# A scan on VectorE for the running sums of log f, key rows copied by DMA, and a new order of the first words, in a fused attention and GELU kernel

## The chip, the cores and the metric

The kernel runs on one core of one Trainium2 chip. The metric is device time in microseconds (us) of one execution. The core has TensorE (PE in the profile, with PEld for its weight loads), VectorE (DVE), ScalarE (ACT), GpSimd (POOL) and SyncE (SP); DMA transfers are issued from the queues of SP, ACT and POOL.

## What is computed

Attention with a decay for 8 batches of 8 heads, 576 positions and 64 dimensions, and behind it a two-layer MLP with the tanh form of GELU over 4608 tokens (512 to 2048 to 512):

```python
log_f = np.log(np.clip(f, 0.0001, 1.0))
cum = np.cumsum(log_f, axis=-1)
scores = scale * q @ k.T + cum[..., :, None] - cum[..., None, :]   # causal
attn = softmax(scores) @ v
x = attn as (tokens, heads * dims)
out = gelu_tanh(x @ w_in) @ w_out
```

Since the softmax divides out what depends on the query alone, the kernel needs of `cum` only exp(-cum) of the keys. It multiplies the values by that weight (`vw`) and uses the weights themselves as the columns of the denominators (`w_bf`).

## The kernel before, in words

Sixteen quads (4 heads of one batch each) run through attention, two quads a batch. For a quad the loads of queries and keys (`LQ.i`, `LK.i`, line 208, on POOL's queue, cast to bf16) are followed by a 32x32 block transpose on DVE (`TQ.i`, `TK.i`, line 214). `S.i.r` or, for two heads, `H.i.r.g` are the score products of a round of columns (line 277, contraction over 32 rows) and their exponentials on ACT (line 285), through two PSUM tiles of the pool psS. `M` masks on POOL (line 291), `m` by a product on DVE (line 321). `VW` and `vw` weight the values (line 231) on POOL or DVE. `D.i` are the denominators (products at lines 333 and 347, then a transpose, a reciprocal and a transpose back on DVE, lines 366 to 370), `V.i.x` and `v.i.x` the products with the values and their division into `xT` (line 379). The first two quads are split into query parts; the third number of their words says which.

From the third quad on, 64 key rows stand in an extra block named LOW: `CL.i` (`copy_low`, line 236) copies rows 0 to 63 of block 0 of `vw` to rows 64 to 127 of block LOW. V reads that block as its second.

The MLP goes by nine chunks of 512 tokens. `I`, `i`, `J` and `j` are whole products with `w_in` (lines 395 and 419), 16 matmuls to a J; `GJ` the GELU that a j left over. `Q`, `E` and `e` are products of sums (Strassen's scheme) with sums from `T`, `UW`, `PW` and `U`. `F.c.n` and `f.c.n` pull n steps of the products with `w_out`: for chunk 0 a step is one block of 128 rows by 512 columns (line 667), for later chunks of 256 columns (line 600). F issues a step as one matmul over the full 128 columns of the array, f as four matmuls over 32 columns each. Results go to DRAM by SP's queue.

`WI.c` and `WO.c` load the pieces of `w_in` and `w_out` (lines 197 and 201) on POOL's queue; J.x.g needs WI.2g and WI.2g+1, and an F of chunk 0 passes through WO.0 to WO.3 in turn. `LP` and `LC` load value tiles on POOL's queue (line 185), `LV` and `LB` on SP's. `B.n.c` is filler: n matmuls of c columns over zeros into an unused tile (line 256). `X` and `Y` load ACT's tables for exp and GELU. `Z` and `TR` or `tr` set zeros and the two causal triangles.

The order of the work on every engine is written out by hand: `run` goes through tables of such words, `SETUP` and `FRONT` once (quads 0 to 6 and chunks 0 and 1 in part), then `SECOND`, `STEADY`, `FLUSH` and `LAST` for the chunks from 2 on, with the quad number moved on by two a chunk. Each engine and each DMA queue takes its instructions in this order; a word with `@` waits for another word's load.

Running sums before: `setup` (from line 677) loads f as 64 rows of 576, clips it on DVE (line 694), takes Ln on ACT (line 695), transposes the five blocks on PE (line 700) and copies them from PSUM to `logfT` on ACT (lines 702 and 703). The word `CW` (`make_w`) then multiplies by a triangle of ones (line 719, within a block) and adds whole blocks by products with ones (line 721), all in fp32, and ACT takes exp(-cum - 64) into `wT` (line 724). `W` casts `wT` to `w_bf` on DVE (lines 748 and 749).

Of the kernel before, what the change touches and what calls it, by code (L numbers as in the profile page):

```python
# [16 lines left out]
def kernel(  # L17
# [49 lines left out]
    LOW, HIGH = NT, NT - 1  # L67
# [4 lines left out]
        TK.0 LP.0 LP.1  # L72
# [74 lines left out]
    f_sb = f_all[0:BH, :]  # L147
# [87 lines left out]
    def copy_low(i):  # L235
        return nc.vector.tensor_copy(vw[i % 2][64:128, LOW], vw[i % 2][0:64, 0])
# [440 lines left out]
    def setup():  # L677
# [10 lines left out]
        nc.vector.memset(logfT, 0.0)  # L688
# [28 lines left out]
    def make_w():  # L717
        cum_ps = psM.tile([128, NT * BH], FP32, name="cum_ps", tag="m")
        nc.tensor.matmul(cum_ps, utri_f32, logfT, start=True, stop=True)
        for n in range(NT - 1, 0, -1):  # L720
            nc.tensor.matmul(cum_ps[:, n * BH:], ones_f32, logfT[:, :(NT - n) * BH], start=False, stop=True,  # L721
                             skip_group_check=True)
        for (rows, t0, t1) in ((128, 0, HIGH), (64, HIGH, NT)):
            nc.scalar.activation(
                wT[:rows, :, t0:t1, :].rearrange("p i t h -> p t i h"),
                cum_ps[:rows, t0 * BH:t1 * BH].rearrange("p (t i h) -> p t i h", i=NQ, h=4),
                AF.Exp, scale=-1.0, bias=shift[:rows, :])
# [131 lines left out]
```

## Time and profile before

| | |
|---|---|
| median of 3 runs | 323.59 us (323.31 to 323.96) |
| profiled execution | 323.22 us |
| its span, first to last instruction | 321.4 us |
| PE, ACT, DVE, POOL busy | 309.6, 212.7, 242.0, 107.8 us |
| granted TensorE clock | 1.00 |

Busy time is the time in which an engine had an instruction in it. Matmuls are pipelined, so the distance from one start to the next says what a matmul costs PE, not its own length. In a row of the timeline stand the start, the length, the engine, the line, the operation, output and input tiles, how many instructions are in the row and, in brackets, how long the engine stood idle before it and what ended that. In the windows each engine's busy time is followed by its instructions, then come the granted clock, the DMA share and GB/s. In the rows of groups, busy time and the mean in ns are followed by the idle time before them. In the rows of DMA issues the last number is the median time from issue to landing in us.

### The profile page before, as it was taken

How to read it: one execution, taken by the hardware profiler on the slowest of the kernel's cores; microseconds unless marked ns; L12 is line 12 of the kernel's file. 1: busy time of each engine (PE TensorE's matmuls, PEld its weight loads, DVE VectorE, ACT ScalarE, POOL GpSimd, SP SyncE). 2: the span in 40 equal slices, each digit the busy share in tenths (PEclk: the TensorE clock that was granted, in tenths of full speed). 3: DMA queues.
4: the chain of work that ended last, by engine and by line, in shares of the span. 5: the costliest groups of instructions: out<-in, count | busy, mean ns of one | idle time of the engine just before them, and what ended most of it. 6: DMA issues, size and time to landing. Idle time of an engine off the chain costs nothing.

```text
span 321.4 us, 11820 instructions
## 1 busy us (share of the span) xinstructions
PE 309.6 (96%) x5339; PEld 220.7 (69%) x5339; DVE 242.0 (75%) x374; ACT 212.7 (66%) x242; POOL 107.8 (34%) x145
## 2 busy tenths in 40 slices
PE   0899999999999999999999999999999999999996
PEld 0557844544776567776788878767776786688785
DVE  4765337898979879779877987699876866597674
ACT  4676576775766776878767866787586744836610
POOL 8989343522301416400851075205610140000000
PEclk9999999999999999999999999999999999999999
DMA  7999999585126931593139411971011111010203
GB/s 126 218 210 208 247 213 199 104 155 109 35 43 129 227 78 37 116 209 72 39 82 228 87 39 35 190 172 36 7 47 53 37 34 37 30 37 0 100 33 99
DMA packets 47490, 33.41 MB, mean 104 GB/s; under 512 B 29776, under 2 KB 42192, under 8 KB 47440
## 3 DMA queue, kind: packets, MB, share of 16 engines
q0 software_dynamic: 9632, 15.99, 28.3%
q1 hardware_dynamic: 37664, 16.60, 19.1%
q8 instruction: 41, 0.67, 0.9%
q14 instruction: 9, 0.07, 0.1%
q10 hardware_dynamic: 144, 0.07, 0.1%
HBM read 36.85 MB, written 9.44 MB: 144 GB/s over the span
## 4 chain that ended last, share of the span: by engine, by line
PE 91%; ACT 3%; DVE 3%; DMA 2%; issue 1%; POOL 0%; DVEq 0%; POOLq 0%
PE ps_w L600 30%; PE ps_h L395 19%; PE ps_s L277 9%; PE po L347 9%; PE ps_q L520 8%; PE pso L667 4%; PE ps_h L419 4%; PE ps_u L468 4%; DMA q_c<-in_q_dram 2%; PE po_m L333 1%; ACT pt L285 1%; ACT gT L403 1%; DVE xT L379 1%; PE idle_ps L256 1%; PE cum_ps L721 1%
## 5 line engine op out<-in xcount | busy, mean ns | idle before, releaser
L285 ACT ACTIVATE pt<-ps_s 128x1024 bf16<-128x1024 f32 (+2 forms) x100 | 94.0, 990 | 38.6 <-PE ps_s L277 35.9
L291 POOL TENSOR_SCALAR_AFFINE_SELECT pt<-pt 128x512 bf16<-128x512 bf16 (+3 forms) x65 | 41.4, 647 | 95.2 <-ACT pt L285 72.3
L395 PE MATMUL ps_h<-xT,w_in_sb 128*128 128x512 bf16 (+1 forms) x320 | 66.8, 358 | 0.3 <-ACT gT L403 0.2
L395 PEld LDWEIGHTS <-w_in_sb 128*128 128x128 bf16 x320 | 31.2, 98 | 26.6 <-issue 0.6
L600 PEld LDWEIGHTS <-gT 128*32 128x32 bf16 (+1 forms) x1216 | 44.1, 97 | 5.5 <-issue 2.2
L403 ACT ACTIVATE gT<-ps_h 128x1024 bf16<-128x1024 f32 x34 | 34.6, 1017 | 18.7 <-PE ps_h L395 18.4
L600 PE MATMUL ps_w<-w_out_sb,gT 128*32 128x256 bf16 (+1 forms) x1008 | 42.6, 273 | 0.0
L277 PE MATMUL ps_s<-qT,kT 32*128 32x64 bf16 (+5 forms) x896 | 36.3, 263 | 3.2 <-DVE qT L214 3.0
L600 PEld LDWEIGHTS <-gsum 128*32 128x32 bf16 (+1 forms) x948 | 35.4, 97 | 3.8 <-issue 1.5
L231 POOL TENSOR_TENSOR vw<-v_nat,wT 128x1280 bf16<-128x1280 f32 (+1 forms) x13 | 29.6, 2279 | 11.7 <-DMA v_nat<-in_v_dram 11.4
L536 DVE TENSOR_TENSOR usnap<-ps_q,usnap 128x1024 f32<-128x1024 f32 x15 | 17.9, 1222 | 18.6 <-PE ps_q L520 13.2
L277 PEld LDWEIGHTS <-kT 32*128 32x128 bf16 x896 | 16.5, 93 | 19.6 <-issue 10.1
L600 PE MATMUL ps_w<-usum,gsum 128*32 128x256 bf16 (+1 forms) x791 | 30.0, 273 | 0.0
L617 DVE COPY snap<-ps_w 128x512 f32<-128x512 f32 x32 | 21.8, 681 | 6.2 <-PE ps_w L600 6.0
L531 ACT ACTIVATE gT<-usnap 128x1024 bf16<-128x1024 f32 x15 | 15.8, 1054 | 12.1 <-DVE usnap L536 11.8
L379 DVE TENSOR_TENSOR xT<-po,rb 128x576 bf16<-128x576 f32 x26 | 19.5, 752 | 5.6 <-PE po L347 5.3
L347 PE MATMUL po<-pt,vw 128*32 128x64 bf16 (+4 forms) x624 | 22.4, 278 | 0.0
L214 DVE STREAM_TRANSPOSE qT<-q_c 128x576 f32<-128x576 f32 x16 | 19.8, 1246 | 1.7 <-DMA q_c<-in_q_dram 1.7
L347 PEld LDWEIGHTS <-vw 128*32 128x32 bf16 x672 | 14.6, 97 | 9.4 <-issue 2.8
L214 DVE STREAM_TRANSPOSE kT<-k_c 128x576 f32<-128x576 f32 x16 | 19.5, 1246 | 1.9 <-DMA k_c<-in_k_dram 1.9
L208 POOL DMA_DIRECT2D k_c<-in_k_dram x16 | 9.1, 568 | 33.6 <-DVE kT L214 18.0
L520 PEld LDWEIGHTS <-w_in_sb 128*128 128x128 bf16 x160 | 15.6, 98 | 2.5 <-issue 0.4
(135 smaller groups left out, 478.5 us busy)
## 6 DMA issues: line engine op xcount, KB each, us to landing
out_dram<-o_st SPq DMA_DIRECT2D x35, 256.0 KB, 2.3
k_c<-in_k_dram POOLq DMA_DIRECT2D x16, 288.0 KB, 5.3
q_c<-in_q_dram POOLq DMA_DIRECT2D x16, 288.0 KB, 6.3
v_nat<-in_v_dram SPq DMA_DIRECT2D x16, 256.0 KB, 5.4
v_nat<-in_v_dram SPq DMA_DIRECT2D x20, 128.0 KB, 5.1
v_nat<-in_v_dram POOLq DMA_DIRECT2D x8, 256.0 KB, 8.1
w_in_sb<-in_moe_w_in_dram POOLq DMA_DIRECT2D x8, 256.0 KB, 7.8
w_out_sb<-in_moe_w_out_dram POOLq DMA_DIRECT2D x4, 512.0 KB, 11.3
```

What stands on the lines that cost most here:

```text
L214: return nc.vector.transpose(out=dst.rearrange("p s c -> p (s c)").bitcast(FP32) .rearrange("p (t a) -> p a t", a=S // 32), in_=src.rearra ...
L231: return eng.tensor_mul(vw[i % 2][:, t0:t1], vb[:, t0:t1, h0:h0 + 4, :], wT[:, i, t0:t1, :].unsqueeze(3).to_broadcast([128, t1 - t0, 4, D]))
L277: nc.tensor.matmul(tiles[h // 2][:, h % 2, c0:c0 + nq], key_columns(i, key, h, c), qq[32 * h:32 * h + 32, q0:q0 + nq, c], start=(c == 0 an ...
L285: nc.scalar.activation(p[:, 2 * g:2 * g + 2, off:off + n], t[:, :, 0:n], AF.Exp, scale=scale)
L291: nc.gpsimd.affine_select(out=x, in_=x, compare_op=ALU.is_ge, fill=0.0, base=0, pattern=pattern, channel_multiplier=-1)
L347: nc.tensor.matmul(po[r0:r0 + w.shape[-1], 448 + q0:448 + q0 + nq], w, p[:, h, col:col + nq], start=(key in (0, "low")), stop=(key in ("lo ...
L379: nc.vector.tensor_mul(xT[:, 2 * u + x, r0 + s0:r0 + s1], po, rbs[i, part])
L395: nc.tensor.matmul(ph[:, j, n * cols:(n + 1) * cols], w_in_sb[:, dt, 128 * ft:128 * ft + 128], xT[:, dt, h0:h0 + cols], start=(dt == 0 and ...
L403: nc.scalar.activation(gelus(c, 2 * pr, 2), ph, AF.Gelu_apprx_tanh)
L520: nc.tensor.matmul(ps[:, k, HC * n:HC * n + HC], w[:, d, 128 * n:128 * n + 128], x[:, d, :], start=(first and n == 0 and d == 0), stop=(d ...
L600: nc.tensor.matmul(ps[c0:c0 + width, n, cols[0]:cols[1]], x[:, j, 128 * n + c0:128 * n + c0 + width], w[:, j, cols[0]:cols[1]], start=(fir ...
L617: copy(kept[name], ps)
```

## The change

Three things change.

1. Running sums: behind Ln one `tensor_tensor_scan` on DVE multiplies the state by one and adds the next element, along the 576 positions of the 64 rows. `CW` becomes the five transposes of the summed rows into PSUM and the same two exponentials on ACT. The ACT copies to `logfT`, its memset and the fp32 products go. `CW` moves into `SETUP`, ahead of the first key transpose.
2. `copy_low` becomes a DMA issued by SP, in every table that has `CL`.
3. `FRONT` has another order. Among it: `TR` on DVE becomes `tr` on ACT; several masks change between POOL and DVE, `VW.1.1` goes to DVE and `vw.2` to POOL; three `UW.2` sums on DVE become `PW.2` on POOL; filler goes from 10 matmuls (3,968 columns) to 30 (8,960 columns); the loads stand in another order and the words with `@` become fewer; F and f steps are split otherwise, with 38 steps of chunk 0 as F before and 40 after, of chunk 1 35 and 22, the sums of F and f being the same (64 and 97).

```diff
     SETUP = """
-        TK.0 LP.0 LP.1
+        CW TK.0 LP.0 LP.1
     """
     FRONT = """
-        Z TQ.0 LP.2 TR WI.1 TQ.1 S.0.0 B.1.384 CW WI.0 TK.1 S.0.2 LP.4 LP.3 B.1.512 vw.0.0 B.2.512 H.1.0.1 H.1.1.1 WI.3 M.0.0 W vw.1.0 WI.2 B.2.512
-        WI.5 LQ.2 WI.4 H.1.0.0 D.0.0 M.1.0.1 M.1.0.0 H.0.1.1 V.0.0.0 H.0.1.0 M.0.1 WI.6 V.0.1.0 B.2.256 H.1.1.0 B.1.256 D.1.0 H.0.3.0 B.1.256 V.1.0.0 H.0.3.1
-        WI.7 LK.2 V.1.1.0 m.0.3.2 H.1.3.0 j.0.0 vw.0.1 H.1.3.1 LC.1.4 WO.0 m.0.3.4 WO.1 D.0.1 M.1.3 S.1.2 M.1.1 VW.1.1 V.0.0.1 V.0.1.1 LC.1.2 D.1.1
-        J.0.1 J.0.2 WO.2 LC.1.0@VW.1.1 WO.3@m.0.3.2 V.1.0.1 V.1.1.1 LC.1.1 GJ.0.0 LC.1.3 TK.2 J.1.1 LK.3 J.0.3 J.1.0 LQ.3 TQ.2 LQ.4 VW.3
-        J.1.3 LK.4 J.1.2 F.0.4 X F.0.4 S.2.0 F.0.11 TK.3 S.2.2 F.0.6 LV.2.0 TQ.3 F.0.4 LK.5 S.2.1 F.0.2 F.0.7 TQ.4 m.2.1 S.3.0 vw.2 CL.2 M.2.2 f.0.7
-        M.2.0 D.2 S.3.1 f.0.7 LQ.5 V.2.0 m.3.0 S.3.2 TK.4 LK.6@LQ.4 f.0.1 f.0.3 V.2.1 M.3.2 f.0.2 S.4.1 CL.3 m.3.1 LQ.6 f.0.5 TQ.5 H.4.2.1 D.3 H.4.0.1
-        H.4.0.0 VW.4 V.3.1 v.3.0 f.0.1 H.4.2.0 U.0 m.4.1 LV.2.1@m.3.1 I.1.1 LQ.7@CL.3 I.1.4 TQ.6 I.1.6 m.4.2.3 I.1.0 m.4.2.2 I.1.5 CL.4 U.3 LV.3.0@LQ.7
-        U.1 TK.6 I.1.2 M.4.0 U.2 G.0 TK.5 UW.2.1 I.1.3 I.1.7 G.1.1.2 F.1.16 X UW.2.2 S.5.0 UW.2.3 LQ.8 F.1.19 S.5.1 D.4 VW.5 M.5.0 f.1.13 S.5.2 V.4.0
-        f.1.14 V.4.1 UW.2.4 m.5.2.3 m.5.2.2 CL.5 M.5.1 S.6.0 f.1.13 D.5 S.6.1 f.1.4 LK.7 V.5.1 f.1.3 f.1.10 vw.6 S.6.2 m.6.1 M.6.2.2 m.6.0 V.5.0
-        LV.3.1@LK.6 f.1.5 CL.6 LK.8 m.6.2.3
+        B.1.256 B.1.128 TQ.0 S.0.0 TK.1 B.1.128 B.1.256 B.2.512 B.1.128 LP.4 B.1.512 B.1.256 B.1.512 LP.2 LP.3 B.1.128 B.1.512 WI.4 TQ.1 vw.0.0 S.0.2 B.1.128 B.1.128 B.1.128 H.0.1.1 H.1.1.1 WI.6 B.1.128 B.1.128 B.1.256 M.0.0 B.1.512 WI.0 WI.1 H.1.0.1 tr W LC.1.4 D.0.0 V.0.1.0 WI.2 B.2.512 B.1.512 B.1.256 vw.1.0 H.1.0.0 V.0.0.0 B.1.256 B.1.128 B.1.256 m.1.0.0 H.0.1.0 H.1.1.0 m.1.0.1 B.1.512 B.1.128 D.1.0 WI.3 Z V.1.0.0 WI.5 LK.2 H.0.3.0 B.1.512 WO.2 B.1.128 M.0.1 WO.1 WI.7 V.1.1.0 H.0.3.1 vw.0.1 vw.1.1 m.0.3.2 H.1.3.1 LC.1.2 j.0.0 S.1.2 M.0.3.4 D.0.1 m.1.1 V.0.0.1 H.1.3.0 m.1.3 LQ.2 J.0.1 TK.2 GJ.0.0 V.0.1.1 D.1.1 WO.0 J.0.2 V.1.0.1 WO.3 LC.1.1 LC.1.0 V.1.1.1 J.1.2 LC.1.3 J.1.1 LK.3 LQ.3 J.0.3 J.1.0 TQ.2 LQ.4 LK.4 J.1.3 F.0.3 VW.3 f.0.1 F.0.1 X TK.3 F.0.3 S.2.0 F.0.9 S.2.2 TQ.3 F.0.2 CL.3 M.2.0 F.0.8 VW.2 F.0.3 S.2.1 F.0.1 M.2.2 F.0.3 M.2.1 F.0.2 f.0.2 TQ.4 F.0.2 LQ.6 S.3.0 f.0.2 CL.2 LQ.5 X f.0.4 TK.4 D.2 S.3.1 f.0.3 m.3.0 f.0.1 V.2.0 f.0.2 S.3.2 TQ.5 F.0.3 LV.2.0 m.3.1 M.3.2 f.0.2 V.2.1 S.4.1 f.0.5 H.4.2.1 UW.2.1 LK.5 D.3 VW.4 H.4.0.0 H.4.0.1 V.3.1 v.3.0 f.0.1 TK.5 M.4.1 f.0.1 LQ.7 H.4.2.0 TQ.6 U.0 LK.6 I.1.7 I.1.3 I.1.5 I.1.4 I.1.2 m.4.2.3 I.1.0 CL.4 I.1.1 U.3 LV.2.1 I.1.6 TK.6 F.1.5 U.1 m.4.2.2 LV.3.0@LQ.7 PW.2.2 G.0 f.1.1 F.1.5 S.5.0 f.1.13 m.4.0 G.1.1.2 LK.8 f.1.8 VW.5 f.1.4 S.5.1 M.5.1 f.1.4 D.4 f.1.2 F.1.6 S.5.2 V.4.0 f.1.1 m.5.2.3 f.1.4 m.5.2.2 f.1.2 CL.5 f.1.7 LV.3.1 V.4.1 M.5.0 PW.2.3 f.1.1 U.2 S.6.0 f.1.5 D.5 f.1.6 m.6.0 LQ.8 f.1.1 S.6.1 f.1.2 V.5.1 f.1.8 LK.7 f.1.2 S.6.2 M.6.2.2 m.6.1 f.1.3 vw.6 V.5.0 M.6.2.3 f.1.1 F.1.5 PW.2.4 F.1.1 CL.6
     """
...
     def copy_low(i):
-        return nc.vector.tensor_copy(vw[i % 2][64:128, LOW], vw[i % 2][0:64, 0])
+        return nc.sync.dma_start(out=vw[i % 2][64:128, LOW], in_=vw[i % 2][0:64, 0])
...
         nc.vector.memset(ones_f32, 1.0)
-        nc.vector.memset(logfT, 0.0)
...
         nc.scalar.activation(f_sb, f_sb, AF.Ln)
         idle_ps.append(psO.tile([128, 1024], FP32, name="idle_ps", tag="po"))
-        ps_lt = psM.tile([128, NT * BH], FP32, name="ps_lt", tag="m")
-        for t in range(NT):
-            n = min(128, S - 128 * t)
-            nc.tensor.transpose(ps_lt[:n, t * BH:(t + 1) * BH], f_sb[:, 128 * t:128 * t + n], ident_f32)
+        nc.vector.tensor_tensor_scan(f_sb, ones_f32[0:BH, 0:1].to_broadcast([BH, S]), f_sb, 0.0,
+                                     op0=ALU.mult, op1=ALU.add)
         run(SETUP)
-        nc.scalar.copy(logfT[:, :HIGH * BH], ps_lt[:, :HIGH * BH])
-        nc.scalar.copy(logfT[0:64, HIGH * BH:], ps_lt[0:64, HIGH * BH:])
...
     def make_w():
         cum_ps = psM.tile([128, NT * BH], FP32, name="cum_ps", tag="m")
-        nc.tensor.matmul(cum_ps, utri_f32, logfT, start=True, stop=True)
-        for n in range(NT - 1, 0, -1):
-            nc.tensor.matmul(cum_ps[:, n * BH:], ones_f32, logfT[:, :(NT - n) * BH], start=False, stop=True,
-                             skip_group_check=True)
+        for t in range(NT):
+            n = min(128, S - 128 * t)
+            nc.tensor.transpose(cum_ps[:n, t * BH:(t + 1) * BH], f_sb[:, 128 * t:128 * t + n], ident_f32)
```

## The prediction

> **What bounds the kernel now.** I read the page's chain first (section 4), then busy time by stage, then the timelines of PE, ACT, DVE and POOL over the first 41 us, where the change acts. All durations are of the profiled execution (323.22 us, span 321.4); the median of the runs shown is 323.59, 0.37 above it, so what I add to the one I add to the other.
>
> ```profile
> PE 91%; ACT 3%; DVE 3%; DMA 2%; issue 1%; POOL 0%; DVEq 0%; POOLq 0%
> ```
> ```profile
> 12.00:21.00 9.00, 8.73 (x132) 4.01 (x131) 6.75 (x15) 8.15 (x12) 8.40 (x13) 1.00 1.14 207
> ...
> 27.00:41.00 14.00, 14.00 (x166) 12.00 (x159) 4.47 (x7) 7.93 (x9) 7.58 (x10) 1.00 1.20 240
> ```
>
> The chain that ended last is PE for 91%. In the windows (columns: PE, PEld, DVE, ACT, POOL busy, granted clock, DMA share, GB/s) 12 to 21 us is different: ACT works 8.15 of 9 us. That is the start, where sixteen exponentials of the first two quads are waited for; from 27 us on PE is full and DMA is at 240 GB/s. So a microsecond saved ahead of the first MLP products (word j.0.0) counts, one saved on DVE, ACT or POOL later does not, and one added to PE later counts in full.
>
> ```profile
> L285 ACT ACTIVATE pt<-ps_s 128x768 bf16<-128x768 f32 x8 | 6.3, 810 | 3.5 <-PE ps_s L277 3.4
> L285 ACT ACTIVATE pt<-ps_s 128x1024 bf16<-128x1024 f32 x4 | 4.0, 1021 | 0.1
> L285 ACT ACTIVATE pt<-ps_s 128x640 bf16<-128x640 f32 x4 | 2.6, 695 | 0.4 <-PE ps_s L277 0.4
> ```
> ```profile
> 9.47 1.51 ACT L285 ACTIVATE pt<-ps_s 128x768 bf16<-128x768 f32 x2 [2.00 <-PE ps_s L277]
> 12.62 0.67 ACT L724 ACTIVATE wT<-cum_ps,shift 128x256 f32<-128x256 f32 x2 [1.64 <-PE cum_ps L721]
> ```
> ```profile
> 8.62 0.83 PE L277 MATMUL ps_s<-qT,kT 32*128 32x256 bf16 x16 [2.96 <-DVE qT L214]
> 9.38 0.50 PE L256 MATMUL idle_ps<-idle 128*128 128x384 bf16 x1
> 9.67 1.27 PE L719 MATMUL cum_ps<-logfT,utri_f 128*128 128x320 f32 x2
> 10.74 1.85 PE L721 MATMUL cum_ps<-logfT,ones_f 128*128 128x64 f32 x8
> 12.52 0.46 PE L277 MATMUL ps_s<-qT,kT 32*128 32x320 bf16 x8
> ...
> 21.50 1.92 PE L419 MATMUL ps_h<-xT,w_in_sb 128*128 128x256 bf16 x16
> ```
>
> The sixteen exponentials are 6.3 + 4.0 + 2.6 = 12.9 us. After the first two ACT stands still 1.64 us for the products of CW; PE has them in front of S.0.2 from 9.67 to 12.52. These 2.85 us look like the prize of the change.
>
> **Part by part. (1) The scan.** It stands between the Ln and the first key transpose.
>
> ```profile
> 3.58 0.45 DVE L694 TENSOR_SCALAR f_all<-f_all 64x576 f32<-64x576 f32 x1 [1.32 <-DMA f_all<-in_f_dram]
> 5.89 1.26 DVE L214 STREAM_TRANSPOSE kT<-k_c 128x576 f32<-128x576 f32 x1 [1.86 <-DMA k_c<-in_k_dram]
> 7.30 1.26 DVE L214 STREAM_TRANSPOSE qT<-q_c 128x576 f32<-128x576 f32 x1 [0.15 <-DMA q_c<-in_q_dram]
> ```
> ```profile
> 4.06 0.68 ACT L695 ACTIVATE f_all<-f_all 64x576 f32<-64x576 f32 x1 [1.97 <-DVE f_all L694]
> ```
>
> Ln ends at 4.74; no scan is in the trace. Over the same 576 elements the DVE rows run from 0.45 (clip) to 1.26 us (transpose); a recurrence hands each element the last result, so I take the slow row, 1.26, which ends at 6.0, 0.1 after the keys land. The key transpose then ends at 7.27, in time for the queries, which land at 7.3: cost nothing, and the cover is 0.03 us. At 0.45 nothing changes; at twice 1.26 the start slips by 1.2 us. [...]
>
> **(2) The products of CW** go from PE, and the five transposes (4.89 to 5.7 now) move behind the scan to about 6.1 to 6.9, where PE waits for the queries anyway. But what stands ahead of S.0.2 instead is filler: the nine B words between S.0.0 and S.0.2 stream 3,456 columns. The one filler there now takes 0.29 us from its start to the next (9.38 to 9.67) for 384 columns, 0.76 ns a column. So S.0.2 starts at 9.38 + 2.63 = 12.0 against 12.52. Of the 2.85 us, 0.5 is left. At full rate (J: 8.75 us for 80 times 256 columns, rows below, 0.43 ns a column) they would take 1.5 us, and S.0.2 would wait for its banks, freed by the first exponentials at 10.3 and 11.0. The filler row speaks for the slow value, though the granted clock reads 1.00 in every window.
>
> **(3) On ACT** the two wT exponentials (0.67) leave the queue ahead of S.0.2, whose first exponential starts at 12.35 (0.33 after its products, as S.0.2 would have allowed now) in place of 13.19, while the three copies of tr come in behind H.1.0.1: by the wT rows 0.3 to 0.47 each, I take 0.8 us (bounds 0.5 and 1.4). One pays the other. What is left is filler that waits beside the exponentials, and slightly less slack between them: I take 0.2 us less until j.0.0. DVE holds against more: vw.0.0 waits for the values, and W and D.0.0 stand behind it.
>
> **(4) Words that load.** j.0.0 needs WI.0 and WI.1, now issued after WI.4 and WI.6. All DMA of POOL is a backlog that lands in order:
>
> ```profile
> 14.49 0.72 POOL L197 DMA_DIRECT2D w_in_sb<-in_moe_w_in_dram  x1
> ```
> ```profile
> w_in_sb<-in_moe_w_in_dram POOLq DMA_DIRECT2D x1, 256.0 KB, 6.7
> ```
> ```profile
> 23.08 0.74 POOL L201 DMA_DIRECT2D w_out_sb<-in_moe_w_out_dram  x1
> ```
> ```profile
> w_out_sb<-in_moe_w_out_dram POOLq DMA_DIRECT2D x1, 512.0 KB, 12.6
> ```
>
> The fourth piece of w_in, with all five values ahead of it, lands at 14.49 + 6.7 = 21.2 now. In the changed order the same bytes stand ahead of WI.1, so it lands at about 21.2 as well: a floor under j.0.0, which starts at 21.50 now. So j.0.0 goes to 21.3: **0.2 us gained**, at most 0.3. WI.7, needed by the fifth of the products that follow, stands behind WO.2 and WO.1; the same bytes but one query load (about 1.4 us) land now with WO.1 at 23.08 + 12.6 = 35.7, so WI.7 lands at 34.3.
>
> ```profile
> 27.16 3.67 PE L419 MATMUL ps_h<-xT,w_in_sb 128*128 128x256 bf16 x32
> 30.76 1.22 PE L333 MATMUL po_m<-pt,vw 128*32 128x320 bf16 x40
> 31.91 8.91 PE L419 MATMUL ps_h<-xT,w_in_sb 128*128 128x256 bf16 x80
> 40.66 1.89 PE L667 MATMUL pso<-w_out_sb,gT 128*128 128x512 bf16 x8
> ```
>
> From j.0.0 to the first F is 19.16 us of PE (21.50 to 40.66) and the set of words is the same. A J is 16 products, 1.75 us; J.0.3 starts 3 x 1.75 = 5.25 us ahead of F, at 35.2: WI.7 has 0.9 us to spare. WO.3 lands no later than now.
>
> **(5) Turns of the array.** Here the new order costs. The row of 19 at 98.8 holds four products of 32 columns (one step of f) and 15 of 128 (F):
>
> ```profile
> 98.82 2.03 PE L600 MATMUL ps_w<-w_out_sb,gsum 128*32 128x256 bf16 x19
> 100.69 0.59 PE L395 MATMUL ps_h<-xT,w_in_sb 128*128 128x512 bf16 x2
> ```
> ```profile
> 131.15 1.48 PE L600 MATMUL ps_w<-usum,gT 128*128 128x256 bf16 x12
> 132.47 1.04 PE L520 MATMUL ps_q<-xT,w_in_sb 128*128 128x256 bf16 x8
> ```
>
> Twelve F steps take 1.32 us, 0.11 each; sixteen would be 1.76, but 98.82 to 100.69 is 1.87. The step from column tiles to the full array costs 0.11. The other way it is the same: 32 J products ahead of V take 3.60 us where 80 pro rata give 3.50. A step of f itself costs what a step of F costs. I count in the FRONT table, from the first F to the end, how often PE goes between score tiles, column tiles and full array: 32 times and once into SECOND before, 41 times after (F.0.3 f.0.1 F.0.1, F.1.5 f.1.1 F.1.5 and the like). One more lies between j.0.0 and F. Nine turns are **1.0 us** of PE that nothing hides. If the turns were hidden behind weight loads it would be 0; by 0.14 it would be 1.3.
>
> **(6) A step moved into a hole.** Ahead of the I products PE waits for DVE:
>
> ```profile
> 65.45 0.75 DVE L379 TENSOR_TENSOR xT<-ps_o,rb 128x576 bf16<-128x576 f32 x1
> ```
> ```profile
> 65.53 0.63 PE L277 MATMUL ps_s<-qT,kT 32*128 32x320 bf16 x8
> ```
>
> I starts at 66.25, as xT ends at 66.2. A second f.0.1 goes between v.3.0 and H.4.2.0: **0.2 us gained**, a step of 512 columns.
>
> **(7) Low key rows on SP, and POOL.** Fourteen DVE copies of 0.22 us go; DVE is off the chain there, so nothing. Each becomes a 32 KB transfer in SP's queue, behind the outputs, and waits there for its VW; behind it wait output stores and value loads. V reads it as its second key block.
>
> ```profile
> L236 DVE COPY vw<-vw x14: 220/221/260, 53.4 to 260.0; 64x256 bf16<-64x256 bf16 x14
> ```
> ```profile
> out_dram<-o_st SPq DMA_DIRECT2D x35, 256.0 KB, 2.3
> ```
> ```profile
> out_dram<-o_st SPq DMA_DIRECT2D x1, 256.0 KB, 6.4
> ```
> ```profile
> 43.76 2.33 POOL L231 TENSOR_TENSOR vw<-v_nat,wT 128x1280 bf16<-128x1280 f32 x1 [6.31 <-DMA v_nat<-in_v_dram]
> ```
>
> Stores take 2.3 us from issue to landing, one (at 51.0, under load) 6.4. In the repeated tables CL.3 has V.2.1, f.0.15, S.4.0, D.3 and f.0.10 ahead of its V, some 4.7 us: hidden. In FRONT VW.2 now runs on POOL behind VW.3 (to 46.1) and a mask, so until about 49.7, CL.2 is issued at 51 and lands at 53.5, ahead of V.2.0 near 56. The three PW sums on POOL (by the vw row, 512 of 1280 columns, 0.9 us each) are read in SECOND. LV.2.0 goes behind a tile of outputs and VW.4 with it; V.4.0 is 25 us later. X ahead of S.5.0 goes, and its table load comes with that exponential itself: nothing.
>
> **The sum:** -0.2 (start) + 1.0 (turns) - 0.2 (hole) = **+0.6 us**: 323.8 in the profiled execution, **324.2** on the median. Own range of this case 323.4 to 325.0. A measurement here can tell about 0.2%, 0.65 us, from no change, so this is the upper edge of no change.
>
> **Rivals.** *The start gains all that the loads allow* (faster). For it: ACT's idle 1.64 us is real, and POOL's zeros (Z) no longer delay a value load, so the stream may land 0.5 to 1 us earlier. Against it: filler, tr and the 21.2 of WI.1. F can't start before WI.7 at 34.3 plus 5.25 = 39.55, or 38.7 with an earlier stream: 1.1 to 2.0 gained; with turns and hole, -0.3 to -1.2, or 322.7 with mostly the latter. *The filler runs at full rate.* [...] Then S.0.2 starts at 11.0 in place of 12.0, but D.0.0 behind W and WI.1 hold j.0.0 at 21.0 to 21.2: 0.1 to 0.3 better than my sum, 324.0, no change. *SP's copy comes late* (slower). Place: V.2.0; it decides from a landing after 56, that is more than 5 us after issue, which the 6.4 us store shows can be; price 0.4 to 1.5 us, 325.2. Against it: LV.2.0, which loaded the queues then, is moved. *The scan is slow* (slower): above 1.28 us everything slips; at twice that 1.2, 325.4.
>
> **How the numbers follow.** My sum 0.46, half of it on either side of the bound (0.25 same, 0.21 slower); full-rate filler 0.12 (0.11 same, 0.01 faster); start gains all 0.21 (faster); late copy 0.11, slow scan 0.10 (slower). So faster 0.22, same 0.36, slower 0.42. The likeliest single case is the sum. The range that leaves out the tails of the first and last rivals is 322.5 to 325.7.
>
> **What would show it.** S.0.2 at 12.0 with filler from 9.4 (at 11.0: the clock); wT ahead of 8 us; the scan's length, and the first query transpose at 7.3; j.0.0 at 21.3; J.0.3 without a wait for WI.7; the first F at 40.6; the first store of the 512-row products and SECOND's first I product about 0.6 to 0.8 us later than 100.7. Wrong if F starts ahead of 40, if steps between F and f cost nothing, or if V.2.0 waits for the low rows.

## The result, and the profile after

| | before | after |
|---|---|---|
| median of 19 runs each, on one chip | 323.78 us (322.90 to 324.65) | 325.11 us (323.72 to 328.21) |
| ratio | | 1.0056, 95% interval 1.0030 to 1.0081 |
| profiled execution, its span | 323.22, 321.4 us | 324.91, 323.0 us |

The changed kernel is slower: by 1.33 us, 0.4%, in the medians and by 0.6% in the ratio, which goes by the means. Five of its 19 runs took 327.6 to 328.2 us and the other 14 have a median of 324.7; none of the 99 runs of the kernel before in this study is above 325.6, so the long runs belong to the change and are told of below.

The chain by engine and the two windows of the changed kernel, as they were shown of before (columns: PE, PEld, DVE, ACT, POOL busy, granted clock, DMA share, GB/s):

```profile
PE 93%; ACT 2%; DMA 2%; DVE 1%; issue 0%; POOL 0%; POOLq 0%
```
```profile
12.00:21.00 9.00, 8.64 (x123) 4.29 (x122) 5.54 (x15) 7.26 (x12) 7.85 (x15) 1.00 1.16 208
27.00:41.00 14.00, 14.00 (x187) 11.81 (x185) 5.72 (x11) 8.43 (x9) 4.83 (x7) 1.00 1.20 230
```

ACT had 8.15 us of work in the 9 us from 12 to 21 us; now it has 7.26, and PE has 93% of the chain. The timelines of DVE, ACT and PE of the changed kernel, in the places that were read of before:

```profile
4.72 1.35 DVE L687 TENSOR_TENSOR_SCAN f_all<-ones_f,f_all 64x576 f32<-64x576 f32 x1 [0.75 <-ACT f_all L685]
...
7.26 1.26 DVE L205 STREAM_TRANSPOSE qT<-q_c 128x576 f32<-128x576 f32 x1
```
```profile
7.01 0.67 ACT L709 ACTIVATE wT<-cum_ps,shift 128x256 f32<-128x256 f32 x2 [1.03 <-PE cum_ps L707]
...
17.02 0.51 ACT L700 CAST causal<-utri_f 128x128 bf16<-128x128 f32 x2
17.55 0.24 ACT L701 CAST causal<-utri_f 64x64 bf16<-64x64 f32 x1
```
```profile
9.34 3.06 PE L247 MATMUL idle_ps<-idle 128*128 128x128 bf16 x10
12.33 0.72 PE L268 MATMUL ps_s<-qT,kT 32*128 32x320 bf16 x8
...
13.84 1.23 PE L268 MATMUL ps_s<-qT,kT 32*128 32x320 bf16 x16 [0.36 <-ACT pt L276]
...
16.47 0.93 PE L247 MATMUL idle_ps<-idle 128*128 128x512 bf16 x4
...
22.25 1.92 PE L410 MATMUL ps_h<-xT,w_in_sb 128*128 128x256 bf16 x16
...
40.87 1.46 PE L658 MATMUL pso<-w_out_sb,gT 128*128 128x512 bf16 x8
...
99.27 0.65 PE L338 MATMUL po<-pt,vw 128*32 128x64 bf16 x20 [0.20 <-issue]
...
102.26 1.03 PE L386 MATMUL ps_h<-xT,w_in_sb 128*128 128x512 bf16 x4
```

The scan takes 1.35 us and wT is ready early, as forecast. But the filler runs from 9.34 to S.0.2 at 12.33, and j.0.0 starts at 22.25, later than the 21.50 of before, although nothing but a wait of 0.36 us stopped PE since 9.34. The first F comes 0.21 us later than before, SECOND's first I 1.57 later, and from there on the distance stays.

Where the time went is seen when the same five points are read from the PE timeline of every kernel of this study. "Full rate" is the first entry in the trace's record of the granted clock. The clock column of the windows reads 1.00 ahead of that entry as well; a lower rate is seen there in the rows, where the same sixteen score products take 1.89 us ahead of it (e6) and 1.23 behind it (after).

| profiled kernel | S.0.0 | full rate from | S.0.0 to j.0.0 | j.0.0 to F | F to I | I to SECOND's I | SECOND's I |
|---|---|---|---|---|---|---|---|
| before | 8.62 | 11.74 | 12.88 | 19.16 | 25.59 | 34.44 | 100.69 |
| after | 8.57 | 13.35 | 13.68 | 18.61 | 26.13 | 35.27 | 102.26 |
| e1 after, 8 turns fewer | 8.33 | 13.61 | 13.68 | 18.61 | 25.69 | 35.98 | 102.28 |
| e2 before, 24 turns more | 8.85 | 12.24 | 13.03 | 19.16 | 26.68 | 35.97 | 103.69 |
| e3 before, scan | 9.59 | 29.10 | 16.78 | 20.46 | 25.59 | 34.64 | 107.06 |
| e4 before, copies on SP | 9.88 | 14.43 | 13.59 | 19.14 | 26.63 | 34.67 | 103.92 |
| e5 after, TR on DVE | 8.84 | 14.25 | 13.72 | 18.64 | 26.13 | 34.88 | 102.21 |
| e6 as e1, values later | 8.59 | 21.04 | 16.58 | 18.66 | 25.69 | 34.64 | 104.15 |
| e7 after, no filler | 8.34 | 19.51 | 15.15 | 18.66 | 26.12 | 34.99 | 103.26 |
| e8 before, scan and filler | 8.75 | 11.86 | 12.36 | 19.14 | 25.58 | 34.80 | 100.64 |
| e9 after, less filler | 9.25 | 29.01 | 17.45 | 19.71 | 26.13 | 35.62 | 108.16 |
| e10 after, early filler | 9.71 | 7.10 | 13.08 | 18.61 | 26.13 | 34.89 | 102.42 |
| e11 as e8, early filler | 8.33 | 6.28 | 12.62 | 19.15 | 25.60 | 34.57 | 100.27 |
| e12 after, all repairs | 8.69 | 6.31 | 12.12 | 19.26 | 25.68 | 35.21 | 100.96 |

S.0.0 itself moves by up to 1.55 us between these executions, with the landing of the first queries. The stretches behind it are what a kernel does, though the one up to j.0.0, and in the latest openings the next as well, also depends on when full rate opens in that execution: e1 and e6 have the same words up to j.0.0 and take 13.68 us with full rate from 13.61 and 16.58 with full rate from 21.04, and e3, with full rate from 29.10, takes 20.46 in the next stretch, where before takes 19.16.

### The profile page after: what moved, and what is told of

It is laid out like the page before. It is cut to its first block, busy times and chain, and to the rows that moved or that the text cites. A ratio compares the mean times of both kernels' runs of the same rounds, so it can differ in the third digit from the quotient of the medians.

```text
span 323.0 us, 11914 instructions
## 1 busy us (share of the span) xinstructions
PE 311.5 (96%) x5382; PEld 219.6 (68%) x5382; DVE 235.3 (73%) x356; ACT 212.8 (66%) x243; POOL 108.9 (34%) x145
## 4 chain that ended last, share of the span: by engine, by line
PE 93%; ACT 2%; DMA 2%; DVE 1%; issue 0%; POOL 0%; POOLq 0%
PE ps_w L591 30%; PE ps_h L386 19%; PE ps_s L268 10%; PE po L338 9%; PE ps_q L511 8%; PE pso L658 5%; PE ps_h L410 4%; PE ps_u L459 4%; PE idle_ps L247 2%; DMA q_c<-in_q_dram 2%; PE po_m L324 2%; ACT pt L276 1%; ACT gT L394 1%; PE ps_p L591 0%; PE ps_o L338 0%
## 5 line engine op out<-in xcount | busy, mean ns | idle before, releaser
L282 POOL TENSOR_SCALAR_AFFINE_SELECT pt<-pt 128x512 bf16<-128x512 bf16 (+3 forms) x62 | 38.6, 632 | 98.8 <-ACT pt L276 76.0
L222 POOL TENSOR_TENSOR vw<-v_nat,wT 128x1280 bf16<-128x1280 f32 x13 | 30.3, 2332 | 8.1 <-DMA v_nat<-in_v_dram 6.3
```

The source lines that it names most:

```text
L222: return eng.tensor_mul(vw[i % 2][:, t0:t1], vb[:, t0:t1, h0:h0 + 4, :], wT[:, i, t0:t1, :].unsqueeze(3).to_broadcast([128, t1 - t0, 4, D]))
L282: nc.gpsimd.affine_select(out=x, in_=x, compare_op=ALU.is_ge, fill=0.0, base=0, pattern=pattern, channel_multiplier=-1)
```

## The experiments

My theory after reading the two traces: the array's turns cost what was forecast, and the rest of the loss lies in the start. Its rivals: the steps between F and f are free and only the start counts; SP's copies cost something; the scan or the missing products cost something. The first four kernels take one part each. The masks and sums that moved between engines were not run by themselves. The tables are long lines, so each edit shows the altered words with their neighbours only.

**e2: turns alone.** The order of before, with steps of F issued as f among F steps in three places.

```diff
-        F.0.4 X F.0.4 S.2.0 F.0.11 TK.3
+        F.0.1 f.0.1 F.0.2 X F.0.1 f.0.1 F.0.2 S.2.0 F.0.2 f.0.1 F.0.2 f.0.1 F.0.2 f.0.1 F.0.2 TK.3
-        F.1.16 X UW.2.2
+        F.1.3 f.1.1 F.1.3 f.1.1 F.1.3 f.1.1 F.1.4 X UW.2.2
-        F.1.19 S.5.1
+        F.1.3 f.1.1 F.1.3 f.1.1 F.1.3 f.1.1 F.1.3 f.1.1 F.1.3 S.5.1
```

> The kernel before with twelve single steps of F turned into f, each between two F, so 24 turns of the array more and nothing else. Turns theory: 24 x 0.11 = 2.6 us slower than before, about 326.4. If turns are hidden behind weight loads: 323.8, no change.

Measured: 326.31 us (5 runs), ratio 1.0070 (1.0056 to 1.0085), so +2.3 us beside its 324.01 of before, 0.096 a turn. F to I grew by 1.09 with ten turns. By this run alone the cost could also be that of f against F, 0.19 us a step; e1 decides between them.

**e1: the changed kernel with eight turns fewer.**

```diff
-        F.0.3 VW.3 f.0.1 F.0.1 X
+        F.0.3 VW.3 F.0.1 F.0.1 X
-        F.0.2 f.0.2 TQ.4
+        F.0.2 F.0.2 TQ.4
-        TQ.5 F.0.3 LV.2.0
+        TQ.5 f.0.3 LV.2.0
-        G.0 f.1.1 F.1.5
+        G.0 F.1.1 F.1.5
-        D.4 f.1.2 F.1.6
+        D.4 f.1.2 f.1.6
```

> The changed kernel with six words of FRONT altered so that F and f no longer alternate next to each other (eight turns of the array fewer, the same steps). Turns theory: 8 x 0.11 = 0.9 us faster than the changed kernel, about 324.2, that is 0.4 above the kernel before; in its profile the first I product of SECOND comes 1.4 us or less after the one of before instead of 1.6, with F start unchanged at 40.9 and 0.9 us less from there on. Start theory (what is lost is lost before the first F, by the array's clock opening later): unchanged, about 325.1. Copy theory (SP's copies): unchanged, about 325.1.

Five words are altered: f becomes F in the first, second and fourth, F becomes f in the others, so five steps more are f.

Measured: 324.84 us (12 runs, one at 327.24), ratio 1.0024 (1.0007 to 1.0042). F to I, where five of the eight turns lie and as many steps are f as before, lost 0.44, as turns would have it, but SECOND's first I did not move, because I to SECOND's I grew to 35.98. PE's timeline of e1 shows why:

```profile
97.33 0.28 PE L591 MATMUL ps_w<-usum,gT 128*32 128x256 bf16 x1
98.74 0.51 PE L591 MATMUL ps_w<-usum,gT 128*32 128x256 bf16 x11 [1.13 <-issue]
```

One product of an f step starts, the next eleven come 1.41 us later, and the idle 1.13 us are put down to "issue": PE waited for nothing that the profile shows, and the weight loads stood as well. The changed kernel has 0.20 us of the same at 99.27. What it is was left to e6, which has the same five words and no such stop: from I to SECOND's I, with three turns fewer and five steps more as f, it takes 34.64 us where e5 takes 34.88. So it is the turns that cost, 0.1 us each, and not the steps of f.

**e3: the scan alone.** Order of before, with `CW` taken out of FRONT and put ahead of TK.0, the scan and its transposes as in the changed kernel.

```diff
-        TK.0 LP.0 LP.1
+        CW TK.0 LP.0 LP.1
-        S.0.0 B.1.384 CW WI.0 TK.1 S.0.2
+        S.0.0 B.1.384 WI.0 TK.1 S.0.2
```

> The kernel before with the scan alone: CW as transposes in SETUP, the fp32 products, the ACT copies and one memset gone, everything else in the order of before. Here nothing stands in the place of the products but one filler of 384 columns. Turns theory: S.0.2 at about 11.0, the first MLP product (now 21.5) about 0.5 to 0.8 us earlier, since its w_in pieces landed at 17.6, and the whole kernel 0.3 to 0.8 faster, 323.0 to 323.5. Start theory: without work on the array its clock opens later, by up to 3 us, and the kernel is as fast as before or up to 1 us slower.

Measured: 329.64 us (4 runs), ratio 1.0175 (1.0156 to 1.0193). Both theories were far off: 5.6 us slower than before, where I had looked for a gain. PE's timeline of e3:

```profile
12.01 0.71 PE L277 MATMUL ps_s<-qT,kT 32*128 32x320 bf16 x6 [0.25 <-ACT pt L285]
...
14.05 1.68 PE L277 MATMUL ps_s<-qT,kT 32*128 32x256 bf16 x16
...
26.37 1.03 PE L419 MATMUL ps_h<-xT,w_in_sb 128*128 128x256 bf16 x4
```

Everything takes longer: sixteen score products 1.68 us, and j.0.0 comes at 26.37. Full rate is granted from 29.10 us only. So a new theory: the fp32 products, which I had taken for a load on PE, kept it busy enough for the clock, and in the changed order the nine B words took this over. Rival: the scan, or the transposes behind it, hold the start back by themselves.

**e8: the same with filler in the place of CW.**

```diff
-        S.0.0 B.1.384 WI.0 TK.1 S.0.2
+        S.0.0 B.1.384 B.6.512 B.1.128 WI.0 TK.1 S.0.2
```

> The kernel before with the scan in place of the fp32 products (as in e3), and 3,200 columns of filler (B.6.512 and B.1.128) where CW stood, so that PE is about as long busy between S.0.0 and S.0.2. Theory of the warm-up: what e3 lost, 5.6 us, came from the products' missing work for the clock and not from the scan; with filler full rate opens by 14 us again, j.0.0 starts at 21.2 to 22, and the time is 323.3 to 324.3. Rival, the scan itself or the transposes behind it hold the start back: the filler changes nothing, full rate opens near 29 us, and the time is 327 to 330.

Measured: 323.37 us (10 runs), ratio 0.9978 (0.9962 to 0.9993). PE's timeline of e8:

```profile
9.51 2.83 PE L256 MATMUL idle_ps<-idle 128*128 128x384 bf16 x8
...
13.56 1.19 PE L277 MATMUL ps_s<-qT,kT 32*128 32x256 bf16 x16
...
21.11 1.92 PE L419 MATMUL ps_h<-xT,w_in_sb 128*128 128x256 bf16 x16
```

Against its own runs of before, e3 was 5.6 us slower and e8 is 0.6 faster, so 6.2 us come back by filler alone. Full rate is there from 11.86, the sixteen score products that took 1.68 us in e3 take 1.19, and this kernel is 0.2% faster than before. The rival falls: the scan costs nothing.

**e7: the changed kernel without its nine B words ahead of S.0.2.**

```diff
-        TK.1 B.1.128 B.1.256 B.2.512 B.1.128 LP.4 B.1.512 B.1.256 B.1.512 LP.2 LP.3 B.1.128 B.1.512 WI.4
+        TK.1 LP.4 LP.2 LP.3 WI.4
```

> The changed kernel without the nine B words (3,456 columns of filler) between S.0.0 and S.0.2. Theory of the warm-up: the array gets full rate only once it has been busy enough, and these fillers took the place of the fp32 products in this; without them full rate opens later than 16 us, j.0.0 starts 1 to 4 us later than 22.25, and the time is 326 to 330. Rival, as the prediction counted: filler only stands in the way of S.0.2; then S.0.2 starts at 10.9 to 11.0, when the first exponentials free its banks, j.0.0 at 21.9, the landing of WI.1, and the time is 324.5 to 324.9.

Measured: 325.89 us (7 runs, one at 330.95), ratio 1.0048 (1.0031 to 1.0066). S.0.2 starts at 10.06, 2.3 us earlier, and j.0.0 at 23.49, 1.24 later: full rate from 19.51. In kind as the warm-up has it; the time lies just below its range. The counting of the prediction, by which this kernel is the better one, falls.

**e5: the casts of the triangles.**

```diff
-        H.1.0.1 tr W LC.1.4
+        H.1.0.1 W LC.1.4
-        WI.4 TQ.1 vw.0.0
+        WI.4 TQ.1 TR vw.0.0
```

> The changed kernel with the three copies of the triangles on DVE again (the capital TR, put behind TQ.1, where DVE stands idle from 12.54 to 14.02 us) in place of ACT. Theory of the casts: in the changed kernel the three casts keep ACT from the exponentials from 17.14 to 17.89 us, so the exponentials run 0.75 us earlier without them, and j.0.0 goes from 22.25 to the landing of WI.1 at 21.9; from S.0.0 to j.0.0 it is 13.3 in place of 13.68, and the time goes from 325.1 to 324.7. Theory of the clock: the start is late because full rate opens at 13.35 us in place of 11.74, whatever ACT does; from S.0.0 to j.0.0 it stays at 13.6 to 13.7, and the time at 325.1.

Measured: 324.64 us (12 runs, four at 327.6 to 329.1), ratio 1.0034 (1.0004 to 1.0064). S.0.0 to j.0.0 is 13.72, as it was. My theory of the casts is refuted. In its trace PE has no wait after 14.10, so what stands in PE's own queue sets j.0.0: between 16.7 and 21.5 us the starts of the rows give 2.00 us of filler (0.86 and three times 0.38), where before has 0.74 (0.32, 0.21, 0.21) in the same place. How much of the later j.0.0 is this filler, and how much the rows that still run at the lower rate until 14.25 (the ten fillers ahead of S.0.2 take 2.99 us from 9.60, where e12 at full rate has 1.57), e5 does not separate.

**e9: less of that filler** (1,280 columns between W and j.0.0 in place of 3,712).

```diff
-        WI.2 B.2.512 B.1.512 B.1.256 vw.1.0
+        WI.2 B.1.512 vw.1.0
-        V.0.0.0 B.1.256 B.1.128 B.1.256 m.1.0.0
+        V.0.0.0 B.1.256 m.1.0.0
-        m.1.0.1 B.1.512 B.1.128 D.1.0
+        m.1.0.1 B.1.256 D.1.0
-        H.0.3.0 B.1.512 WO.2 B.1.128 M.0.1
+        H.0.3.0 B.1.256 WO.2 M.0.1
```

> The changed kernel with 1,280 columns of filler between W and j.0.0 in place of 3,712 (the kernel before has 1,024 there). e5 took the casts from ACT and from S.0.0 to j.0.0 it stayed at 13.7 us, with PE never idle from 12.6 us on. Theory of the filler: PE's own queue sets j.0.0, since these words stand in it; with 2,400 columns less (1.0 us at full rate) j.0.0 comes 13.0 to 13.4 us after S.0.0, the landing of WI.1 (21.9) then being the floor, and the time is 324.6 to 324.9. Rival, the late opening of full rate sets it: 13.6 to 13.7 us, time 325.1.

Measured: 324.69 us (13 runs), ratio 1.0012 (1.0001 to 1.0024) over the nine runs at 323.85 to 324.96; four took 329.2 to 332.6. (The 1,024 columns that the expectation names for before count from D.0.0; from W on before has 2,048.) The nine, with a median of 324.48, come out a little below the forecast of the theory of the filler and not at the 325.1 of its rival, but the profiled execution was one of the others: full rate from 29.01, j.0.0 at 26.70. So the share of these 2,400 columns in j.0.0 was not read from a trace and stays argued. The trace shows the other side of filler instead: with less of it the clock, once late, stays late for longer (29.01 us, where e6 with the full filler has 21.04).

**e6: no turns, and the values loaded later,** that is the edit of e1 and the one below. In e1 and in the changed kernel five value loads (LV.3.1) and a quad's queries and keys are issued between 88 and 92 us; before issues the values from 98.6 on.

```diff
-        CL.5 f.1.7 LV.3.1 V.4.1
+        CL.5 f.1.7 V.4.1
-        vw.6 V.5.0 M.6.2.3
+        vw.6 V.5.0 LV.3.1 M.6.2.3
```

> The changed kernel with eight turns fewer (as in e1), and LV.3.1, five value loads, moved from ahead of V.4.1 to behind V.5.0, where the kernel before has it. In e1 PE stood still for 1.1 us at 97.6 us with neither products nor weight loads and without a wait that the profile shows, right behind a stretch (92 to 97 us) in which the loads fill the DMA engines. Theory of the loads: with the loads elsewhere this stop goes, SECOND's first I product comes at 101.2 in place of 102.28, and the time is 323.7 to 324.0, where e1 took 324.84. Rival, the stop belongs to the order of the words (or to the number of instructions), not to the loads: it stays at 0.2 to 1.1 us, I at 102.2, time 324.8.

Measured: 324.32 us (12 runs, three at 326.8 to 327.8), ratio 1.0023 (0.9994 to 1.0052). The stop is gone: I to SECOND's I is 34.64, 1.34 less than in e1 and as in the kernels with the order of before (34.44 to 34.80). What the stop may have waited for is seen in the DMA view of the same stretch, 91.9 to 96.3 us (queue, kind: packets, MB, share of 16 engines), first of before, then of e1:

```profile
q8 instruction: 2, 0.03, 3.2%
q0 software_dynamic: 7, 0.01, 1.7%
```
```profile
q0 software_dynamic: 276, 0.57, 81.3%
q1 hardware_dynamic: 300, 0.07, 9.2%
```

Before fetches two blocks of 16 KB of instructions there, at 92.20 and 95.96 us by the trace; in e1 queues 0 and 1 fill 90% of the engines and no block is fetched between 90.91 and 96.38. PE goes on at 98.74, 2.4 us after that late block began. If the late block is the cause, it cost PE up to 1.13 us here; the DMA view does not say for which engine a block is. The other traces fit the late block in part. Four have a stop put down to "issue" in this stretch: the changed kernel, e1, e9 and e12, of 0.20, 1.13, 0.37 and 0.35 us. In each PE goes on 2.2 to 2.4 us after the start of a block that began 4.8 to 5.5 us behind the one ahead of it, where before has 3.8. But e10 and e5 have distances of 5.29 and 4.83 us without a stop, and e12 a stop though its loads are moved. So moving the loads does not always remove it, and that the late block is the cause stays argued, since no run changed the blocks alone.

The profiled execution of e6 took 326.82 us, and its rows are the best view there is of what the five long runs of the changed kernel may be; of those five none was profiled. Up to j.0.0 its words are the same:

```profile
9.35 3.06 PE L247 MATMUL idle_ps<-idle 128*128 128x128 bf16 x10
...
13.85 1.89 PE L268 MATMUL ps_s<-qT,kT 32*128 32x320 bf16 x16 [0.36 <-ACT pt L276]
...
18.15 1.67 PE L247 MATMUL idle_ps<-idle 128*128 128x512 bf16 x4
...
25.16 1.92 PE L410 MATMUL ps_h<-xT,w_in_sb 128*128 128x256 bf16 x16
```

The sixteen score products take 1.89 us where the changed kernel's profile has 1.23, the four fillers 1.67 where it has 0.93, and j.0.0 comes 2.9 us later. Full rate begins at 21.04 in place of 13.35, though PE's rows show no more than 0.36 us of standing still since 8.59.

**e4: SP's copy alone,** in the order of before.

```diff
-        return nc.vector.tensor_copy(vw[i % 2][64:128, LOW], vw[i % 2][0:64, 0])
+        return nc.sync.dma_start(out=vw[i % 2][64:128, LOW], in_=vw[i % 2][0:64, 0])
```

> The kernel before with copy_low as a DMA on SP and nothing else. Turns theory: the repeated tables hide it; in FRONT the order of before puts CL.2 behind the value loads LV.2.0 and right behind vw.2, some 2.7 us ahead of its use, so there it can be late: V.2.0 waits 0 to 2 us for it, 323.8 to 325.5, and nothing elsewhere. Copy theory: slower by more than 1 us in several places, CL of the repeated tables among them.

Measured: 326.20 us (8 runs, one at 329.57), ratio 1.0076 (1.0047 to 1.0105). The waits of PE and the timeline around V.2.0:

```profile
PE po L347 <- DMA vw<-vw: 0.9, 1, 0.9
```
```profile
58.06 0.39 PE L347 MATMUL po<-pt,vw 128*32 128x512 bf16 x4
59.31 0.65 PE L347 MATMUL po<-pt,vw 128*32 128x64 bf16 x20 [0.86 <-DMA vw<-vw]
```

V.2.0 waits 0.86 us for the low rows, and F to I grows by 1.04. The rest of its loss in the profiled execution, 1.96 us by F, lies in the start: S.0.0 1.26 later, because the queries landed later, and full rate later with it. The first copy is issued at 55.33 us, so nothing in the trace ties this late start to it. But the median of the eight runs lies 2.2 us above before and outside my range, and beyond the 1.04 the cause stays open. From SECOND's first I to the end the distance to before grows by 0.2 us only (3.23 to 3.43), so the copies of the repeated tables are hidden, as forecast. In the changed order the copy is issued at 51.48, lands 2.1 us later and V.2.0 at 56.38 does not wait: the rival of the prediction is real, but the new order avoids it.

**e10: early filler for the changed kernel,** to make the clock sure.

```diff
-        CW TK.0 LP.0 LP.1
+        B.11.512 CW TK.0 LP.0 LP.1
-        B.1.256 B.1.128 TQ.0 S.0.0
+        B.1.256 B.1.128 B.2.512 B.1.256 TQ.0 S.0.0
```

> The changed kernel with more filler ahead of the first scores: B.11.512 ahead of CW (PE waits there for the scan until 6.2 us) and B.2.512 B.1.256 ahead of S.0.0 (PE waits there for the queries). Theory of the warm-up: full rate opens when a window of some 3.4 us was busy enough, wherever the windows fall; in the changed kernel a quarter of the runs miss it once or twice (325 us, but 327 to 328 then). With this filler full rate is there by 8.6 us in every run, S.0.2 starts at 10.9 to 11.1 in place of 12.33, no run is above 326, and the median is 324.3 to 324.8, as WI.1 (21.9) holds j.0.0. Rival, the runs at 327 to 328 have another cause: a quarter of them stays there, and S.0.2 at 12.3.

Measured: 324.48 us (12 runs), ratio 1.0014 (1.0005 to 1.0024); one run at 330.16. Full rate comes early, at 7.10, but is taken away again. The windows of e10 (the clock is the third number from the end):

```profile
7.20:10.40 3.20, 1.40 (x24) 0.81 (x23) 1.94 (x3) 0.71 (x3) 2.78 (x5) 1.00 1.05 207
10.60:13.80 3.20, 3.20 (x19) 1.23 (x17) 1.74 (x2) 1.36 (x3) 2.14 (x5) 0.50 1.07 211
```

PE waited 1.8 us for late queries, was busy for 1.40 of 3.20 us, and in the next window the granted clock is 0.50; the record goes from open to closed to open again in steps of 3.413 us. S.0.2 starts at 12.86, not at 11. The long runs became fewer (one of 12 for five of 19), which is too few to call them gone; that early filler was undone here by the thin stretch behind it is my reading of the two windows.

**e11: early filler for e8.**

```diff
-        CW TK.0 LP.0 LP.1
+        B.11.512 CW TK.0 LP.0 LP.1
-        TQ.1 S.0.0 B.1.384
+        TQ.1 B.2.512 B.1.256 S.0.0 B.1.384
```

> e8 (the order of the kernel before with the scan and filler for the products) with the same early filler as e10. Its WI.0 and WI.1 land at about 17.6 us. Theory of the warm-up: full rate by 8.6 us, S.0.2 by 11.1 in place of 12.27, and the exponentials, which set this stretch, run 1.0 to 1.3 us earlier; j.0.0 at 19.8 to 20.4 in place of 21.11, time 322.2 to 322.7. Rival, the values or the weights hold j.0.0 at 20.9 to 21.1: time 323.2 to 323.5.

Measured: 323.01 us (7 runs, one at 328.5), ratio 0.9967 (0.9955 to 0.9980). S.0.2 starts at 10.40, as expected, but the next scores wait for the second quad's keys:

```profile
10.40 0.50 PE L277 MATMUL ps_s<-qT,kT 32*128 32x320 bf16 x8
...
13.31 0.96 PE L277 MATMUL ps_s<-qT,kT 32*128 32x256 bf16 x16 [1.65 <-DVE kT L214]
...
20.95 1.92 PE L419 MATMUL ps_h<-xT,w_in_sb 128*128 128x256 bf16 x16
```

So the rival was right about j.0.0, which gains 0.2 us, though not about what holds it: it is DVE's key transpose at 12.02, behind a query transpose that waits for its load until 10.92, and not the values or weights. The time lies between the two theories.

**e12: the changed kernel with all repairs:** the edits of e1, e6, e9 and e10 together.

> The changed kernel with the repairs together: eight turns fewer, LV.3.1 behind V.5.0, the early filler of e10 and the smaller filler of e9; scan, SP's copies and all other words as in the changed kernel. If the losses found are separate and all of them: j.0.0 at 21.9 (WI.1), first F at 40.5, I at 66.2, SECOND's first I at 100.8, time 323.2 to 323.7, no run above 326. Rival, something else of the new order costs as well (SP's copies, the words ahead of I): I later than 66.6 or SECOND's I later than 101.3, time above 324.

Measured: 325.45 us (12 runs, 323.43 to 328.07), ratio 1.0050 (1.0019 to 1.0080). The profiled execution, 323.67, came out as the sum has it: F at 40.07, I at 65.75, SECOND's I at 100.96, with a stop of 0.4 us left in the last stretch. But five of the 12 runs took 326.7 to 328.1, at a mean granted clock of 0.978 to 0.984 (1.000 in the profiled one), so in them the clock was closed for a time after it had opened; that less filler behind the early opening lets it close is my reading, as none of the five was profiled. The repairs add up where the clock holds, and it holds less often. The best version found stays e11 (one of its seven runs was long), or e8, which needs no early filler and had no long run in ten.

One thing is left untested: all kernels with the new order of the start also have SP's copies. The copies begin at 47 us or later, behind the late start that e6 shows, so I do not count them as its cause, but that order with DVE's copies was not run.

## Why the prediction was right or wrong

The measured 325.11 lies inside the range and on the side that had most of the chance; the time named, 324.2, was 0.9 low. As a difference it is +1.33 us in the medians for a forecast of +0.6. The part with the mechanism right is the turns; the start had the wrong sign, one loss was not foreseen, and the long runs were not either. That the time is inside the range all the same is in part luck. Point by point:

- **(1) Scan:** right. 1.35 us for 1.26, the key transpose ends at 7.23, and the query transpose starts with its data at 7.26. e8 shows the scan free.
- **(2) Filler ahead of S.0.2:** 12.33 for 12.0 (2.99 us for 2.63). What failed is the reading "what stands ahead of S.0.2 instead is filler", as mere time: e3, e7 and e8 show that the time of full rate goes with the products, and then with the filler: it begins at 11.74 us with the products and at 29.10 without them (e3), at 11.86 with filler in their place (e8), and in the new order at 13.35 with the nine B words and at 19.51 without (e7). Taken away, they cost 5.6 us in e3; in the new order, if e6's long profile stands for the five long runs, they suffice in 14 of 19. This is what the prediction lacked. Its rival, the filler at full rate, failed too: S.0.2 came at 12.33 and not at 11.0, and with more filler in all full rate began at 13.35 in place of 11.74, and in e6 at 21.04. Five of 19 runs some 3.2 us longer are 0.85 us in the mean, more than the whole forecast, and 0.4 in the median (325.11 against 324.7 without them).
- **(3) "I take 0.2 us less until j.0.0":** failed by its size and place. The casts take 0.75 us, close to the 0.8, and e5 shows that they cost nothing. The filler between D.0.0 and j.0.0 was counted as waiting beside the exponentials; it stands in PE's queue with 2.00 us for 0.74, and S.0.0 to j.0.0 grew by 0.80. That the filler makes up most of this is argued (e9).
- **(4) Loads:** WI.1 landed at 21.88 for 21.2, WI.7 at 33.60 for 34.3, without a wait. In e12 j.0.0 starts at 20.81 and its third product waits for WI.1, which lands at 21.64: this is the floor, and it lies under the third product and not under the first. Between j.0.0 and F the forecast was a turn more, +0.11; it is 0.55 less, since the same rows of scores and value products take 3.16 us there for 3.80. So F came at 40.87 for 40.6, by two errors that cancel, which is luck.
- **(5) Turns:** right. 0.096 each in e2. Of the eight turns that e1 and e6 take out, five save 0.44 from F to I, and three save 0.24 from I to SECOND's I (34.88 in e5 to 34.64 in e6), 0.085 each.
- **(6) The hole:** it is closed as forecast, but the gain does not show. The last score products ahead of I hold PE for 0.56 us (66.43 to 66.99), where 0.72 passed before (65.53 to 66.25), 0.16 less. Yet e1, with this step moved and as many turns from F to I as before, takes 25.69 for 25.59. What costs the other 0.26 us there is open.
- **(5) and (6) together** were to be 0.8 us from F to SECOND's I. F to I grew by 0.54. From I to SECOND's I it is 0.26 between 34.88 and the mean of the five kernels in the order of before, 34.62: 0.80. The total fits, but by e1 and e6 it is made up of 0.68 for the eight turns and 0.12 for all the rest, hole included.
- **(7) Copies:** right for this order (e4 shows the price in the other, and no price in the repeated tables). Not foreseen: the value loads that move ahead of V.4.1 and the stop of 0.2 to 1.1 us behind them.

So 1.57 us in the profiled execution are: start to F 0.21, turns and hole together 0.80, and 0.57 in the last stretch (rounded). Of these 0.39 lie between the changed kernel and e5 (35.27 against 34.88), with the stop of 0.20 as the part that the trace shows, and 0.18 are that the profile of before was at its lowest there (34.44 against 34.62).

Each turn cost 0.085 to 0.11 us in these runs. What PE does in that time no run here shows.

## What to carry to other kernels

Before work is taken from TensorE ahead of a dense stretch, look at what rate it runs at. Here products that looked like waste were what full rate went with: it began at 11.74 us with them, at 29.10 without, at 11.86 with filler in their place. A replacement has to do the same in every execution and not only in the profiled one: the same words had full rate from 13.35 us in one profile (after) and from 21.04 in another (e6). Count how often PE goes between products over the full array and over 32 columns, which cost 0.085 to 0.11 us each here. And where DMA is filled while PE runs short instructions, look whether instruction blocks still arrive: in e1 none was fetched for 5.5 us and PE stopped for 1.13 us, though that the one caused the other was not shown.

## What the runs showed of the hardware

- The granted clock changes in steps of 3.413 us in these traces, called windows here. From its last opening on, the record of each of the 14 traces holds full rate for 300.373, 303.786, 310.613, 314.026 or 317.440 us, which are 88, 89, 91, 92 and 93 times 3.4133 us, and in e10 it was open, closed and open again in steps of 3.413. The opening falls at another phase in each execution: 13.35, 13.61 and 14.25 us in the changed kernel, e1 and e5, whose words on PE are the same up to there. Unbroken work in a window was not enough: in e6 PE stood still for 0.36 us between 8.59 and 21.04, and not at all in the window from 14.21 to 17.63, and full rate came at 21.04 only. So busy time in the profile was not what decided here.
- What fits is how much of the array the work uses. This is an estimate of mine from the starts and sizes in the traces: add up the columns that the products stream in a window, each weighted by the share of the array's rows and columns in use (a product over 32 rows or 32 columns is a quarter), an fp32 column counted as two (320 of them take 0.53 us where 384 of bf16 take 0.29). The 14 windows that opened the clock first hold 3,050 to 3,740. The windows ahead of them hold at most 2,940, but for one in e9 with 3,120. In e5 the window that opened ended 5.41 us behind S.0.0 and holds 3,050; in e6 one that ended 5.62 behind holds 2,940 and did not. By this count the same words can miss the opening by the phase alone, and two windows more at the lower rate, from 14.21 to 21.04, are what e6's profile shows. A limit near 3,000 is no more than this count, and e9's window speaks against a sharp one.
- A scan over 64 rows of 576 fp32 elements takes 1.35 us. A copy of 32 KB by SP's DMA within the on-chip memory takes 2.4 us from issue to landing in the median of 14 (1.7 to 4.7), where DVE's took 0.22.
